# Four PSUM banks for the coarse exponentials, and four moved pieces, in a state-space convolution and feed-forward block

## The chip, the core and the metric

The kernel runs on one core of a Trainium2 chip. A core has TensorE (PE in the profile; PEld is its weight load), VectorE (DVE), ScalarE (ACT), GpSimd (POOL) and SyncE (SP), which issues the DMA transfers here. Each engine takes its instructions in the order of the program, and engines wait for one another on semaphores. TensorE writes to PSUM, which has eight banks of 128 partitions by 512 float32. The metric is the device time of one execution in microseconds (us); lower is better.

## The reference, cut to what matters

Two blocks in a row, each with a layer norm whose shift, scale and gate come from a small modulation vector:

```
mod = silu(c) @ w_mod                      # sa, ca, ga, sb, cb, gb
h = layernorm(x) * (1 + ca) + sa
x = x + ga * (S4 convolution of h)         # 512 channels, 2048 steps
h = layernorm(x) * (1 + cb) + sb
x = x + gb * (mish(h @ w1 + b1) @ w2)      # 512 -> 1792 -> 512
```

The convolution kernel of a channel is K[l] = Re sum over n of C[n] dB[n] exp(dt A[n] l), n = 0..127, l = 0..2047, with complex A, B, C. The output is the causal convolution of K with h, plus a skip term h * Dskip. It is computed with transforms over the 2048 steps; the transformed input is multiplied with the transformed K, and the product is transformed back. Mish is x * tanh(softplus(x)). All of it is in float32.

## The kernel before, in words

The program has three stages. The first, up to about 270 us, builds K for 512 channels and the transform of the normalised input. The second, up to about 365 us, multiplies the transforms and goes back. The third is the feed-forward block on TensorE, to the end. The change is in the first stage alone.

**Parameters.** The 512 channels make four blocks of 128 (b = 0..3). `params(b, stage)` turns a block's A, B, C, dt into the logarithm of a magnitude and an angle for every pole (lines 233-298); it runs on DVE, but for a logarithm and an exponential (stage 1) and an arctangent (stage 4) on ACT. Stage 5 writes the result, split in a rounded part and a rest, to the tile `pk`, of which there is one; `store_pk(b)` sends it to DRAM, and `load_s(b)` (line 546) brings it back in another layout: `S3` (magnitudes, one buffer) and two parts of `S12` (angles, three slots). Blocks 0, 1 and 2 are prepared ahead of the loop, block 3 inside it.

**Chunks.** A block is eight chunks of 16 channels, k = 0..31. For a chunk the kernel needs exp(z l) for 32 fine and 64 coarse values of l. The pieces of a chunk, with their names in the code and in the trace:

- `coarse(k, h)`, h = 0, 1: one product of 64x512 on PE (`pco`) into a PSUM bank, and its exponential on ACT into `co`. All 16 of a block are done in one go, `visit(b)`, since the exponential and the sines need different ACT tables. A visit is: load the exponential's table, 16 times product and exponential, load the sines' table.
- `s_ang` (PE, `pang`, 8 products) and `s_sin` (ACT, three passes: absolute value, sine, cosine) give the sines and cosines of the fine values in `ec`.
- `s_mag` and `comb` (DVE) multiply them with the magnitudes. `s_mag` is one 128x512 product into `m`. `comb` is four operations on `ec`: a product of 128x1024 with `co`, two of 128x512 with `m`, and one of 128x992 with `co`.
- `s_kgen` (PE, `pkg`, 64 small products into a bank), `s_ks` (ACT, a copy to `ks`), `s_skip` (DVE, adds the skip term to 4 columns of `ks`), `s_ka` (PE, `pka`, 16 products), `s_tm` (ACT, a copy to `gk`).

**The input's side.** The steps come in eight tiles of 256 (n = 0..7). `u_load` loads one, `u_stats(n)` (n even) takes the mean and variance of two tiles: 20 DVE operations (four statistics of 128x512, four aggregations, twelve of 128x4 for the inverse root). `u_norm(n)` is four DVE operations of 128x512, `u_mm` and `u_out` are products on PE (`pua`) and copies on ACT.

**The order.** It is written by hand: `follow` chains every instruction of PE, DVE, ACT and the SP loads in the order in which the code issues them. The loop (line 639) does at step k, on PE: `s_kgen(k-1)`, `s_ang(k+3)`, `s_ka(k-3)`, and what the table `pe` adds; on ACT and SP: `s_ks(k-1)`, what the table `se` adds, `s_sin(k+2)`, `s_tm(k-3)`; on DVE: the list `own`, between whose members the operations of the table `ve` ("extras") are spread evenly, and then those of `vt`. Calls such as `at(ve, 11, params, 3, 5)` fill the tables. `own` was:

```
own = comb(k) if 0 < k < NG else []
own.insert(1, lambda: step(s_skip, k - 2))
if k % 8 != 7:
    own.append(lambda: step(s_mag, k + 1))
```

so that the skip addition of chunk k-2 was the second DVE operation of step k. `s_kgen(k)` runs one step after `comb(k)` and needs all four of its operations. After steps 7, 15 and 23 comes the next visit; visit 0 is ahead of the loop.

**PSUM.** The eight banks are divided by tag: `pa` two pairs (`pang`), `pu` two single banks, `pb` two single banks. Before, all `pco` and `pua` take `pu`, while `pkg`, `pka` and `pmod` take `pb`. During a visit no other product runs on PE.

Of the kernel before, what the change touches and what calls it, by code (L numbers as in the profile page):

```python
# [10 lines left out]
F32 = mybir.dt.float32  # L11
F32R = mybir.dt.float32r
# [6 lines left out]
P = 128  # L19
# [65 lines left out]
def s4_block(ctx, tc, io, out):  # L85
# [9 lines left out]
    pre = p0.enter_context(tc.tile_pool(name="pre", bufs=1))  # L95
# [3 lines left out]
    psum = ps.enter_context(tc.tile_pool(name="psum", bufs=2, space=bass.MemoryType.PSUM))  # L99
# [3 lines left out]
    def follow(eng, ins):  # L103
        if eng in order:
            tc.add_manual_dep(ins.ins, order[eng].name,
                              mybir.DependencyInfo(mybir.DependencyClass.NoSync, mybir.DependencyReason.DATA),
                              reason="program order")
        order[eng] = ins.ins
# [31 lines left out]
    def act(out, in_, f, **kw):  # L140
        follow("act", nc.scalar.activation(out, in_, f, **kw))  # L141

    def tables(name):
        follow("act", nc.scalar.preload_act_table_set(name))

    def mm(out, lhsT, rhs, start=True, stop=True):
        follow("pe", T.matmul(out, lhsT, rhs, start=start, stop=stop))  # L147

    def load(dst, src):
        follow("sp", nc.sync.dma_start(dst, src))  # L150

    pkd = dram.tile([NB, P, 12 * P], F32, name="pkd")
# [4 lines left out]
    def pair(tag, name, bufs=None):  # L157
        return psum.tile([P, 2, 512], F32, tag=tag, name=name, **({"bufs": bufs} if bufs else {}))
# [4 lines left out]
    def view(src, offset, ap):  # L163
        return bass.AP(tensor=src.tensor, offset=src.offset + offset, ap=ap)
# [14 lines left out]
    def load_params(b):  # L179
        raw[b] = gen.tile([P, 16, P], F32, tag="raw" if b % 2 else "ec", name=f"raw{b}", bufs=1 if b % 2 else 3)  # L180
        load(raw[b][:, 0:6, :], io["par"][b].rearrange("p (k n) -> p k n", k=6))
# [118 lines left out]
    CO, S3 = {}, {}  # L300

    def coarse(k, h):
        if h == 0:
            CO[k] = gen.tile([P, 16, NM], F32, tag="co", name=f"co{k}", bufs=9)
        p = psum.tile([P, 512], F32, tag="pu", name=f"pco{k}{h}")
        mm(p[:, :8 * NM], S3[k // 8][:, k % 8, :], mc[:, h, :])
        act(CO[k][:, 8 * h:8 * h + 8, :].rearrange("p d x -> p (d x)"), p[:, :8 * NM], AF.Exp)

# [3 lines left out]
    def s_ang(k, half=None):  # L312
        if half != 1:
            PA[k] = pair("pa", f"pang{k}")
        s = S12[k // 4 % 3][:, k % 4]
        for e in range(2) if half is None else (half,):
            for n in range(4):
                rhs = ac[:, n // 3, :] if n % 3 == 0 else am[:, n - 1:n].to_broadcast([96, 512])
                mm(PA[k][:, e, :], s[:, e, :], rhs, start=(n == 0), stop=(n == 3))

    def s_sin(k):
        EC[k] = gen.tile([P, 2, 16, 96], F32, tag="ec", name=f"ec{k}", bufs=3)
        pv = PA[k].rearrange("p e (d x) -> p e d x", d=16)
        ang = [EC[k][:, z].rearrange("p d (e x) -> p e d x", x=32)[:, 0:3:2] for z in range(2)]
        A.activation(ang[0], pv, AF.Abs)
        act(ang[1], pv, AF.Sin, scale=-TWO_PI)
        act(ang[0], ang[0], AF.Sin, scale=-TWO_PI, bias=halfpi)
# [121 lines left out]
    def u_stats(n):  # L449
        v = Later()  # L450
        s6 = conv.tile([P, 4, 6], F32, tag="bst", name="bst", bufs=2)
        for h in range(4):
            v.bn_stats(s6[:, h], XT[n + h // 2][:, h % 2])
        for h in range(4):
            v.bn_aggr(mv[:, 2 * n + h, :], s6[:, h])
        rsqrt(rstd[:, 2 * n:2 * n + 4], mv[:, 2 * n:2 * n + 4, 1], 4, conv, "rsq", v)
        return v.ops
# [59 lines left out]
    def run(*lists):  # L517
        for i in range(max(map(len, lists))):
            for ops in lists:
                if i < len(ops):  # L520
                    ops[i]()
# [21 lines left out]
    def store_pk(b):  # L543
        load(pkd[b], PKR[b].rearrange("p i e n -> p (i e n)").bitcast(F32))

    def load_s(b):
        S3[b] = pre.tile([64, 8, P], F32R, tag="s3", name=f"s3_{b}")
        load(S3[b].bitcast(F32), view(pkd, P * b * 12 * P + 2 * P, [[3 * P, 64], [16 * 12 * P, 8], [1, P]]))
        for h in range(2):
            load(S12[(2 * b + h) % 3][0:64].bitcast(F32),  # L550
                 view(pkd, (P * b + 64 * h) * 12 * P, [[3 * P, 64], [16 * 12 * P, 4], [1, 2 * P]]))

    store_pk(0)
    load_s(0)
    for k in range(0, KB, 2):
        load(early[:, k:k + 2], view(io["w_mod"], k * P * 6 * D, [[6 * D, P], [P * 6 * D, 2], [1, 3 * D]]))
# [12 lines left out]
    def step(f, *a):  # L569
        if f.__name__[:2] == "s_":  # L570
            if (f, *a) in done or not 0 <= a[0] < NG:
                return
            done.add((f, *a))
            if a[1:] == (1,):
                done.add((f, a[0]))
        f(*a)

    def visit(b, others={}):
        tables("natural_log_exp_and_others")
        for i in range(16):  # L580
            coarse(8 * b + i // 2, i % 2)
            run(others.get(i, []))
        if b == 1:
            run(params(3, 1))
        tables("trig_and_small")

    s_ang(0)
    s_ang(1)
    s_sin(0)
    run(params(1, 4), params(2, 4))  # L590
    s_sin(1)
    run(params(1, 5))
    store_pk(1)
    load_params(3)
    run(params(2, 5))
    visit(0, {2: [lambda: step(s_mag, 0), lambda: run(comb(0))], 4: [lambda: step(s_mag, 1)]})
    store_pk(2)
    s_ang(2)
# [2 lines left out]
    pe, se, ve, vt = {}, {}, {}, {}  # L601

    def at(d, k, f, *a):
        d.setdefault(k, []).append((f, *a))

    at(pe, 0, mod_mm)
    at(se, 1, mod_out)
    at(ve, 1, u_stats, 0)
    at(ve, 3, gains)
    for b in range(NB - 1):  # L610
        at(se, 8 * b + 1, load_s, b + 1)
# [1 line left out]
    at(ve, 5, params, 3, 2)  # L613
    at(ve, 9, params, 3, 3)
    at(se, 11, run, params(3, 4))
    at(ve, 11, params, 3, 5)
    at(se, 12, store_pk, 3)
    for n, k, d in ((0, 4, ve), (1, 7, vt), (2, 10, ve), (3, 12, ve), (4, 15, vt), (5, 17, ve), (6, 20, ve), (7, 23, vt)):
        if n % 2 == 0 and n:
            at(ve, 8 if n == 2 else k - 1, u_stats, n)  # L620
# [18 lines left out]
    for k in range(NG + 1):  # L639
        tc.cur_priority = 100000 + 10000 * k  # L640
        for s in [(s_kgen, k - 1), (s_ang, k + 3), (s_ka, k - 3)] + pe.get(k, []):
            step(*s)
        for s in [(s_ks, k - 1)] + se.get(k, []) + [(s_sin, k + 2), (s_tm, k - 3)]:
            step(*s)
        own = comb(k) if 0 < k < NG else []
        own.insert(1, lambda: step(s_skip, k - 2))
        if k % 8 != 7:
            own.append(lambda: step(s_mag, k + 1))
        extra = [o for f, *a in ve.get(k, []) for o in f(*a)]
        for i, o in enumerate(own):  # L650
            o()
            for e in extra[len(extra) * i // len(own):len(extra) * (i + 1) // len(own)]:
                e()
        for f, *a in vt.get(k, []):
            run(f(*a) or [])
        if k % 8 == 7 and k + 1 < NG:
            visit(k // 8 + 1)
            step(s_mag, k + 1)
# [23 lines left out]
    psum = ps.enter_context(tc.tile_pool(name="psum1", bufs=2, space=bass.MemoryType.PSUM))  # L682
# [59 lines left out]
    psum = ps.enter_context(tc.tile_pool(name="psum2", bufs=4, space=bass.MemoryType.PSUM))  # L742
# [163 lines left out]
```

## Time and profile before

| | us |
|---|---|
| median of three runs (lowest, highest) | 733.49 (732.96, 736.34) |
| the profiled execution, its own time | 735.84 |
| its span, first to last instruction | 734.1 |
| outside the span | 1.74 |

| busy in the span | PE | DVE | ACT |
|---|---|---|---|
| 734.1 us | 648.6 | 412.4 | 323.7 |

Times of rows are us from the start of the span. A row of the timeline is: start, duration, engine, line, operation, what is written from what is read, shapes, how many instructions are merged into it; in brackets the idle time of that engine just before, and who ended it. Nearly all rows of the first stage have the line of a helper (L119, L141, L147, L150), so tiles tell them apart. PEclk is the share of the full TensorE clock that was granted; in this trace it is 1.0 or 0.5, in pieces of about 3.4 us.

The four visits are at 38 to 50 us, 95 to 107, 158 to 170 and 215 to 227, by ACT's rows of `co`.

### The profile page before, as it was taken

The page shows a single profiled execution, that of the slowest core. Times are in us where ns is not written, and L with a number is a line of the kernel's source. Part 1 is how long each engine was busy: PE and PEld are TensorE (multiplying, and loading weights), DVE is VectorE, ACT ScalarE, POOL GpSimd, SP SyncE. Part 2 cuts the span into 40 slices and gives each one's busy share as a digit, 9 for nine tenths or more (in the row PEclk, how much of TensorE's full clock was granted, in tenths as well). Part 3 has the DMA queues.
Part 4 walks back from the last instruction along what each step waited for, and adds up shares of the span by engine and source line. Part 5 has one row for each costly group of instructions (what it writes and reads, how often), then busy time and mean ns, then how long its engine had stood idle before and what let it go on. Part 6 is the DMA issues. An engine that isn't in the chain of part 4 may idle for free.

```text
span 734.1 us, 11767 instructions
## 1 busy us (share of the span) xinstructions
PE 648.6 (88%) x4848; PEld 437.5 (60%) x4848; DVE 412.4 (56%) x813; ACT 323.7 (44%) x466; POOL 5.0 (1%) x12
## 2 busy tenths in 40 slices
PE   0489879889979988999737999999999999999996
PEld 0246646546646752333206877887788877888884
DVE  8788978996884837786548224432424324431113
ACT  2477687687986863353305312322123222322220
POOL 2000000000000000000000000000000000000000
PEclk9959958887985999999976999999999999999998
DMA  7841123522423268995275522032500500010002
GB/s 188 272 136 61 45 71 104 188 87 77 142 88 115 100 178 251 300 298 182 115 200 171 116 57 58 1 65 50 114 1 1 115 0 1 0 40 19 0 1 58
DMA packets 34313, 74.62 MB, mean 102 GB/s; under 512 B 5418, under 2 KB 9902, under 8 KB 33748
## 3 DMA queue, kind: packets, MB, share of 16 engines
q1 hardware_dynamic: 33380, 72.17, 33.9%
q10 hardware_dynamic: 576, 1.05, 0.7%
q0 software_dynamic: 304, 0.66, 0.4%
q8 instruction: 38, 0.62, 0.4%
q14 instruction: 15, 0.12, 0.1%
HBM read 49.73 MB, written 24.13 MB: 101 GB/s over the span
## 4 chain that ended last, share of the span: by engine, by line
PE 50%; DVE 3%; DMA 2%; issue 0%; ACT 0%; SPq 0%; DVEq 0%; ACTq 0%
PE pm L795 22%; PE po L812 21%; PE pz L147 2%; PE pia L760 2%; PE pub L147 2%; PE pkb L147 1%; DMA zl<-zd 1%; PE pln L780 1%; DVE ot L119 1%; DVE y L119 0%; DVE w2l L119 0%; DMA zd<-z 0%; DVE x L119 0%; DMA out<-ot 0%; DVE rsq L119 0%
## 5 line engine op out<-in xcount | busy, mean ns | idle before, releaser
L795 PE MATMUL pm<-hh,w1h 128*128 128x512 f32 x448 | 143.2, 400 | 0.7 <-ACT hh L119 0.7
L141 ACT ACTIVATE mh<-pm,b 128x512 f32<-128x512 f32 x56 | 38.6, 689 | 229.7 <-PE pm L795 229.7
L119 DVE TENSOR_TENSOR mal<-mh,mah 128x512 fp32r<-128x512 f32 x56 | 38.7, 691 | 156.8 <-ACT mah L119 156.4
L795 PEld LDWEIGHTS pm<-hh,w1h 128*128 128x128 f32 x448 | 85.3, 190 | 21.8 <-ACT hh L119 1.5
L812 PE MATMUL po<-w2h,mah 128*128 128x512 f32 x224 | 89.4, 399 | 0.0
L795 PE MATMUL pm<-hh,w1l 128*128 128x512 f32 x224 | 89.3, 399 | 0.0
L812 PE MATMUL po<-w2l,mah 128*128 128x512 f32 x224 | 88.6, 395 | 0.0
L812 PE MATMUL po<-w2h,mal 128*128 128x512 f32 x224 | 88.5, 395 | 0.0
L147 PE MATMUL pang<-ac,s 96*128 96x512 f32 x128 | 55.0, 476 | 27.2 <-DMA s<-pkd 27.2
L119 DVE TENSOR_TENSOR ec<-ec,co 128x1024 f32<-128x1024 f32 x64 | 76.9, 1201 | 1.8 <-ACT ec L141 1.8
L147 PE MATMUL pco<-mc,s 64*128 64x512 f32 x64 | 39.8, 708 | 17.1 <-ACT co L141 17.1
L119 DVE TENSOR_TENSOR y<-pkb,f 128x1024 f32<-128x1024 f32 x32 | 37.7, 1219 | 25.1 <-PE pkb L147 25.1
L147 PEld LDWEIGHTS pkg<-ec 128*32 128x32 f32 x2048 | 34.9, 114 | 28.2 <-issue 18.9
L812 PEld LDWEIGHTS po<-w2h,mah 128*128 128x128 f32 x224 | 42.1, 188 | 14.6 <-ACT mah L119 4.9
L147 PEld LDWEIGHTS pang<-ac,s 96*128 96x128 f32 x128 | 28.6, 224 | 34.7 <-issue 27.6
L795 PEld LDWEIGHTS pm<-hh,w1l 128*128 128x128 f32 x224 | 42.6, 190 | 10.1
L812 PEld LDWEIGHTS po<-w2h,mal 128*128 128x128 f32 x224 | 42.1, 188 | 10.2
L812 PEld LDWEIGHTS po<-w2l,mah 128*128 128x128 f32 x224 | 42.1, 188 | 9.8
L147 PE MATMUL pkg<-ec 128*32 128x64 f32 x2048 | 39.6, 230 | 7.1 <-DVE ec L119 5.3
L147 PE MATMUL pang<-am,s 96*128 96x512 f32 x128 | 45.3, 441 | 0.0
L147 PEld LDWEIGHTS pco<-mc,s 64*128 64x128 f32 x64 | 16.9, 269 | 38.9 <-ACT co L141 38.0
L141 ACT ACTIVATE co<-pco 128x512 f32<-128x512 f32 x64 | 35.5, 595 | 10.2 <-PE pco L147 9.5
(97 smaller groups left out, 863.0 us busy)
## 6 DMA issues: line engine op xcount, KB each, us to landing
ud<-u SPq DMA_DIRECT2D x16, 512.0 KB, 3.4
ur<-ud SPq DMA_DIRECT2D x32, 256.0 KB, 4.5
zd<-z SPq DMA_DIRECT2D x16, 512.0 KB, 4.0
zl<-zd SPq DMA_DIRECT2D x28, 256.0 KB, 4.9
x<-in_A_u SPq DMA_DIRECT2D x32, 128.0 KB, 3.3
x<-in_A_u SPq DMA_DIRECT2D x8, 512.0 KB, 6.6
out<-ot SPq DMA_DIRECT2D x32, 128.0 KB, 2.3
w1s<-in_B_w SPq DMA_DIRECT2D x8, 448.0 KB, 6.5
```

Of the source, the lines that this page charges most:

```text
L119: ins = getattr(self.engine, name)(*a, **kw)
L141: follow("act", nc.scalar.activation(out, in_, f, **kw))
L147: follow("pe", T.matmul(out, lhsT, rhs, start=start, stop=stop))
L760: T.matmul(p[64 * tl:64 * tl + 64, :], di, ZL[tt, hv][:, j % 2, tl, :], start=True, stop=True)
L780: T.transpose(p[:, P * q:P * q + P], LNX[tt, q][:, P * b:P * b + P], ident)
L795: T.matmul(p, w1[wi][:, k, fs], hh[:, hi, k, :], start=(n == 0), stop=(n == 3 * KB - 1))
L812: T.matmul(PO[tt][q], a[ai][:, P * q:P * q + P], w2[wi][:, f, :], start=(f == 0 and n == 0), stop=(f == FB - 1 and n == 2))
```

## The change

Five edits, all in the first stage.

1. `coarse(k, h)` takes a bank of the tag `pb` for even k, and of `pu` for odd k. A visit's products go round four banks in place of two.
2. `load_s` issues the two loads of `S12` ahead of the load of `S3`.
3. Ahead of the loop, the arctangents of blocks 1 and 2 stand before `s_sin(0)` on ACT, and no more between `s_sin(0)` and `s_sin(1)`.
4. `u_stats(0)` runs ahead of visit 0, as a whole, and no more between the operations of step 1. The last stage of block 3's parameters (`params(3, 5)`) and its store move one step later, from 11 and 12 to 12 and 13.
5. In `own`, the last operation of `comb` (128x992) becomes the second, and the skip addition comes after all four operations of `comb`.

```
 def coarse(k, h):
-    p = psum.tile([P, 512], F32, tag="pu", name=f"pco{k}{h}")
+    p = psum.tile([P, 512], F32, tag="pu" if k % 2 else "pb", name=f"pco{k}{h}")
...
 def load_s(b):
-    S3[b] = pre.tile([64, 8, P], F32R, tag="s3", name=f"s3_{b}")
-    load(S3[b].bitcast(F32), ...)
     for h in range(2):
         load(S12[(2 * b + h) % 3][0:64].bitcast(F32), ...)
+    S3[b] = pre.tile([64, 8, P], F32R, tag="s3", name=f"s3_{b}")
+    load(S3[b].bitcast(F32), ...)
...
 s_ang(1)
+run(params(1, 4), params(2, 4))
 s_sin(0)
-run(params(1, 4), params(2, 4))
 s_sin(1)
...
 run(params(2, 5))
+run(u_stats(0))
 visit(0, ...)
...
-at(ve, 1, u_stats, 0)
...
-at(ve, 11, params, 3, 5)
-at(se, 12, store_pk, 3)
+at(ve, 12, params, 3, 5)
+at(se, 13, store_pk, 3)
...
 own = comb(k) if 0 < k < NG else []
-own.insert(1, lambda: step(s_skip, k - 2))
+if own:
+    own.insert(1, own.pop())
+own.append(lambda: step(s_skip, k - 2))
```

**First place: ACT ahead of visit 0.** Here `raw1` and `raw2` are the parameters of blocks 1 and 2 (their arctangent), `pang0` and `ec0` the angles and sines of chunk 0. Before:

```order
L119 ACTIVATE ec0_302<-pang0_284 128x2x16x32
L141 ACTIVATE ec0_302<-pang0_284 128x2x16x32
L141 ACTIVATE ec0_302<-ec0_302,halfpi_100 128x2x16x32
L141 ACTIVATE raw1_152<-raw1_152 128x128
L141 ACTIVATE raw2_154<-raw2_154 128x128
L119 ACTIVATE ec1_308<-pang1_293 128x2x16x32
```

and now:

```order
L141 ACTIVATE raw1_152<-raw1_152 128x128
L141 ACTIVATE raw2_154<-raw2_154 128x128
L119 ACTIVATE ec0_304<-pang0_284 128x2x16x32
L141 ACTIVATE ec0_304<-pang0_284 128x2x16x32
L141 ACTIVATE ec0_304<-ec0_304,halfpi_100 128x2x16x32
L119 ACTIVATE ec1_308<-pang1_293 128x2x16x32
```

The two arctangents stand ahead of the first sines.

**Second place: DVE around chunk 1.** `x0`, `x1` are the tiles of the input, `bst`, `mv`, `rsq` and `rstd` belong to `u_stats(0)`, `m2_1` is chunk 1's `m`. Before:

```order
L119 TENSOR_TENSOR m2_1_354<-co1_337 128x512
L119 TENSOR_TENSOR ec1_308<-ec1_308,co1_337 128x32x32
L119 BN_STATS bst_486<-x0_201 128x6 x2
L119 BN_STATS bst_486<-x1_206 128x6 x2
L119 BN_AGGR mv_134<-bst_486 128x2 x2
L119 TENSOR_TENSOR ec1_308<-ec1_308,m2_1_354 128x16x32
L119 BN_AGGR mv_134<-bst_486 128x2 x2
L119 TENSOR_SCALAR rsq_487<-mv_134 128x4
L119 TENSOR_SCALAR rstd_135<-rsq_487 128x4
L119 SCALAR_TENSOR_TENSOR ec1_308<-ec1_308,m2_1_354 128x16x32
```

and now, with the statistics ahead of `m2_0`, further up:

```order
L119 TENSOR_TENSOR m2_1_377<-co1_360 128x512
L119 TENSOR_TENSOR ec1_308<-ec1_308,co1_360 128x32x32
L119 TENSOR_TENSOR ec1_308<-ec1_308,co1_360 128x32x31
L119 TENSOR_TENSOR ec1_308<-ec1_308,m2_1_377 128x16x32
L119 SCALAR_TENSOR_TENSOR ec1_308<-ec1_308,m2_1_377 128x16x32
L119 TENSOR_TENSOR m2_2_513<-co2_373 128x512
```

Nothing is left between the four operations of `comb(1)`; the 20 of `u_stats(0)` are now in front of the first operation that needs `co`.

**Third place: DVE at steps 11 and 12.** `raw3` and `pk3` are block 3's parameters, which wait for the arctangent that ACT does at step 11; `ks9` is the skip addition. Before:

```order
L119 TENSOR_TENSOR ec11_1164<-ec11_1164,co11_967 128x32x32
L119 SCALAR_TENSOR_TENSOR raw3_320<-raw3_320 128x128
L119 TENSOR_TENSOR ks9_1242<-ks9_1242,dtap_86 128x4
L119 SCALAR_TENSOR_TENSOR raw3_320<-raw3_320 128x128
L119 TENSOR_TENSOR ec11_1164<-ec11_1164,m2_11_1266 128x16x32
L119 TENSOR_SCALAR raw3_320<-raw3_320 128x128
L119 SCALAR_TENSOR_TENSOR ec11_1164<-ec11_1164,m2_11_1266 128x16x32
L119 SCALAR_TENSOR_TENSOR raw3_320<-raw3_320 128x128
L119 TENSOR_TENSOR ec11_1164<-ec11_1164,co11_967 128x32x31
L119 CAST pk3_1341<-raw3_320 128x3x2x128
```

and now:

```order
L119 TENSOR_TENSOR ec11_1164<-ec11_1164,co11_967 128x32x32
L119 TENSOR_TENSOR ec11_1164<-ec11_1164,co11_967 128x32x31
L119 TENSOR_TENSOR ec11_1164<-ec11_1164,m2_11_1266 128x16x32
L119 SCALAR_TENSOR_TENSOR ec11_1164<-ec11_1164,m2_11_1266 128x16x32
L119 TENSOR_TENSOR ks9_1242<-ks9_1242,dtap_86 128x4
L119 TENSOR_TENSOR m2_12_1337<-co12_974 128x512
L119 TENSOR_TENSOR ec12_1253<-ec12_1253,co12_974 128x32x32
L119 SCALAR_TENSOR_TENSOR raw3_320<-raw3_320 128x128
L119 TENSOR_TENSOR ec12_1253<-ec12_1253,co12_974 128x32x31
L119 SCALAR_TENSOR_TENSOR raw3_320<-raw3_320 128x128
```

The operations on `raw3` stand one step further down, the skip addition behind the four of `comb`.

More of the change, by code (lines that the diff above doesn't have):

```diff
@@ L546, in load_s @@
     def load_s(b):
-        S3[b] = pre.tile([64, 8, P], F32R, tag="s3", name=f"s3_{b}")
-        load(S3[b].bitcast(F32), view(pkd, P * b * 12 * P + 2 * P, [[3 * P, 64], [16 * 12 * P, 8], [1, P]]))
         for h in range(2):
@@ L551, in load_s @@
                  view(pkd, (P * b + 64 * h) * 12 * P, [[3 * P, 64], [16 * 12 * P, 4], [1, 2 * P]]))
+        S3[b] = pre.tile([64, 8, P], F32R, tag="s3", name=f"s3_{b}")
+        load(S3[b].bitcast(F32), view(pkd, P * b * 12 * P + 2 * P, [[3 * P, 64], [16 * 12 * P, 8], [1, P]]))
     store_pk(0)
```

## The prediction

> **What bounds the kernel now.** I read the page's busy shares first, then TensorE's waits, then the windows by clock, then the timeline around a visit.
>
> ```profile
> PE 648.6 (88%) x4848; PEld 437.5 (60%) x4848; DVE 412.4 (56%) x813; ACT 323.7 (44%) x466; POOL 5.0 (1%) x12
> ```
>
> TensorE sets the end. The windows by stage say where it does not run at its best:
>
> ```profile
> 95.20:115.70 20.50, 18.20 (x106) 10.29 (x106) 16.89 (x46) 14.76 (x25) 0.00 (x0) 0.50 0.16 39
> ...
> 139.50:146.40 6.90, 6.90 (x32) 3.96 (x34) 6.90 (x11) 4.51 (x7) 0.00 (x0) 0.51 0.72 227
> ...
> 160.00:173.70 13.70, 13.66 (x83) 7.17 (x84) 7.72 (x12) 11.85 (x19) 0.00 (x0) 0.50 0.16 39
> ...
> 214.60:235.10 20.50, 17.86 (x106) 10.29 (x106) 10.20 (x14) 14.58 (x23) 0.00 (x0) 0.50 0.29 103
> ...
> 390.00:734.00 344.00, 335.59 (x1448) 263.12 (x1448) 117.27 (x217) 90.05 (x138) 0.00 (x0) 0.98 0.19 43
> ```
>
> After the length come PE's, PEld's, DVE's, ACT's and POOL's busy time, then the granted clock. From 390 us PE is busy for 335.6 of 344 us: nothing of the change is there, and that part only moves as a block. In the visits the clock is half. The waits from 34 us to 260 us, and the timeline of visit 1:
>
> ```profile
> ACT co L141 <- PE pco L147: 9.5, 27, 0.4
> DVE raw L119 <- ACT raw L141: 7.4, 2, 4.3
> PE pkg L147 <- DVE ec L119: 5.3, 4, 1.9
> ```
>
> ```profile
> 95.65 1.08 ACT L141 ACTIVATE co<-pco 128x512 f32<-128x512 f32 x2
> 97.13 1.08 ACT L141 ACTIVATE co<-pco 128x512 f32<-128x512 f32 x2 [0.39 <-PE pco L147]
> ...
> 106.01 1.09 ACT L141 ACTIVATE co<-pco 128x512 f32<-128x512 f32 x2 [0.40 <-PE pco L147]
> ...
> 105.18 1.28 PE L147 MATMUL pco<-mc,s 64*128 64x512 f32 x2 [0.20 <-ACT co L141]
> 106.39 1.96 PE L147 MATMUL pkg<-ec 128*32 128x64 f32 x64
> ...
> 109.72 1.06 PE L147 MATMUL pang<-ac,s 96*128 96x512 f32 x2
> 110.58 1.05 PE L147 MATMUL pang<-am,s 96*128 96x512 f32 x2
> ...
> 115.81 1.17 PE L147 MATMUL pkg<-ec 128*32 128x64 f32 x64
> 120.98 1.17 PE L147 MATMUL pkg<-ec 128*32 128x64 f32 x64
> ```
>
> With two banks the two engines take turns: a pair of exponentials every 1.48 us (97.13 - 95.65), of which ACT works 1.09 and waits 0.39 for products that could only begin when a bank was read. Between visits a chunk takes 5.17 us at the full clock (120.98 - 115.81) and 9.42 at half (115.81 - 106.39), without a gap on PE.
>
> **Edit 1, four banks.** An exponential of mean 595 ns in pairs of 1.09 starts every 0.49 us. At half clock products of 512 columns follow one another at 0.43 us ((110.58 - 109.72) / 2): PE can keep ACT fed when it may be four ahead. So 16 exponentials take 15 x 0.49 + 0.60 = 8.0 us instead of 106.01 + 1.09 - 95.65 = 11.45: ACT leaves 3.5 earlier. PE's last product now needs the 12th exponential, not the 14th: it ends 6.75 us after the first exponential's start (11 x 0.49 + 0.60, a 0.1 hand-over, 0.65 for the product) instead of 10.74 (106.39 - 95.65): **4.0 per visit** on PE. Below, this term is bounded by 0: for even k the bank is shared with `pkg` and `pka`, and `s_tm` must have read it. That copy stands right ahead of the table load, whose 1.28 us cover it here; if they did not, the ring would start a product late. Above, 4.0 plus what a full clock would bring (rivals).
>
> A rule speaks against this term: the Trainium skill, TensorE: Matmul & The Clock Gate, section "HAM oscillation — how this bites in real kernels", reports that adding PSUM double-buffering to a kernel of its own gave no further gain. By that, edit 1 is worth 0 and the time is that of the second rival; the 27 waits of 0.39 above say otherwise.
>
> **Edits 2 and 3, ahead of visit 0.**
>
> ```profile
> 22.00 1.95 SPq L150 DMA_DIRECT2D s<-pkd  x3
> ...
> 29.53 0.35 DVE L119 TENSOR_SCALAR raw<-raw 128x128 f32<-128x128 f32 x2
> 30.95 1.02 ACT L119 ACTIVATE ec<-pang 128x1024 f32<-128x1024 f32 x1 [8.49 <-PE pang L147]
> 33.82 0.51 ACT L141 ACTIVATE raw<-raw 128x128 f32<-128x128 f32 x2
> 34.16 0.62 DVE L119 SCALAR_TENSOR_TENSOR raw<-raw 128x128 f32<-128x128 f32 x2 [4.27 <-ACT raw L141]
> 34.22 1.02 ACT L119 ACTIVATE ec<-pang 128x1024 f32<-128x1024 f32 x1
> 38.50 1.09 ACT L141 ACTIVATE co<-pco 128x512 f32<-128x512 f32 x2
> ```
>
> One load issue is 0.65 us (1.95 / 3), so the first angles come up to 0.65 earlier. The arctangents' input is ready at 29.88, so they end at 30.4, while ACT still waits for angles; the sines start there, 0.55 earlier, and the 0.40 between the two chunks' sines (33.82 to 34.22) falls away. Gain 0.95 (0.4 if the load lands no earlier). The later `load_s` calls I cost at 0: their angles are used four and more steps later. On SP the last such load now waits for block 3's store, with two loads of `w_mod` behind it that have ten steps' time.
>
> **Edit 4, the statistics.** DVE gets the arctangents at 30.4 instead of 34.16 and is done with the parameters 3.7 earlier, at 39.6 instead of 43.3; then come the 20 operations of `u_stats(0)`. Interleaved, they cost 4.6 (below: 8.78 - 4.17); in one piece, where each small one waits for the one before, I take 5.3. So the first `s_mag` starts at 44.9, 1.6 later than before.
>
> ```profile
> 43.29 0.68 DVE L119 TENSOR_TENSOR m<-co 128x512 f32<-128x512 f32 x1
> ...
> 56.76 1.22 DVE L119 TENSOR_TENSOR ec<-ec,co 128x1024 f32<-128x1024 f32 x1
> ...
> 60.51 0.17 DVE L119 TENSOR_TENSOR ks<-ks,dtap 128x4 f32<-128x4 f32 x1 [2.19 <-ACT ks L119]
> ...
> 71.43 1.22 DVE L119 TENSOR_TENSOR ec<-ec,co 128x1024 f32<-128x1024 f32 x1
> ...
> 78.20 1.22 DVE L119 TENSOR_TENSOR ec<-ec,co 128x1024 f32<-128x1024 f32 x1
> ...
> 76.50 1.16 PE L147 MATMUL pkg<-ec 128*32 128x64 f32 x64 [1.88 <-DVE ec L119]
> ...
> 88.42 1.17 PE L147 MATMUL pkg<-ec 128*32 128x64 f32 x64
> ```
>
> From there DVE needs 56.76 - 43.29 - 4.6 = 8.9 to chunk 2's first product: 53.8. To chunk 4's it took 14.67, of which 2.19 was the skip addition waiting for a copy; edit 5 puts that wait behind the products, where the copy is there. 53.8 + 12.5 = 66.3, 5.1 earlier than 71.43. That step takes 6.77 (78.20 - 71.43); the chunk's four products end some 4.7 into it (the rest are the operations behind them), at 71.0, and `pkg` of chunk 4 starts there and not at 76.50. PE, ahead by 0.95 and 4.0, comes there at 69.7 at the latest (76.50 - 1.88 - 4.95), so it waits 1.3 or more for DVE. The next products are done at 66.3 + 6.77 + 4.2 = 77.3, and with one more chunk of PE, 5.17, `pkg` of chunk 6 starts at 82.5 and not at 88.42: **5.9** (5.3 if the clock drops to half after that wait, as in the window at 139.5).
>
> **Edit 5 and the arctangent of block 3, between visits 1 and 2.**
>
> ```profile
> 97.38 1.22 DVE L119 TENSOR_TENSOR ec<-ec,co 128x1024 f32<-128x1024 f32 x1
> ...
> 109.35 0.17 DVE L119 TENSOR_TENSOR ks<-ks,dtap 128x4 f32<-128x4 f32 x1 [1.57 <-ACT ks L119]
> ...
> 127.42 0.29 DVE L119 SCALAR_TENSOR_TENSOR raw<-raw 128x128 f32<-128x128 f32 x1 [3.14 <-ACT raw L141]
> ...
> 138.00 1.15 PE L147 MATMUL pkg<-ec 128*32 128x64 f32 x64 [1.94 <-DVE ec L119]
> ...
> 139.70 1.22 DVE L119 TENSOR_TENSOR ec<-ec,co 128x1024 f32<-128x1024 f32 x1
> 143.87 1.22 DVE L119 TENSOR_TENSOR ec<-ec,co 128x1024 f32<-128x1024 f32 x1
> ...
> 151.52 1.17 PE L147 MATMUL pkg<-ec 128*32 128x64 f32 x64
> 152.65 1.23 DVE L119 TENSOR_TENSOR ec<-ec,co 128x1024 f32<-128x1024 f32 x1
> ```
>
> A plain step is 4.17 on DVE, one with statistics 8.78. PE gains 5.9 + 4.0 = 9.9 by the end of visit 1. DVE starts chunk 8 when two exponentials are done, so 5.9 earlier, at 91.5, and goes to chunk 14 in 46.49 less the waits of 1.57 and 3.14: 133.3. Chunk 14's four products with 10 statistics among them take 6.7: 140.0. PE would be there at 137.7, so **DVE bounds this stretch**: the gain at `pkg` of chunk 14 is 151.52 - 140.1 = 11.4, and the stall of 1.94 before it becomes stalls of some 1.2 and 2.3. Half clock after such a stall cost the chunk at 138.00 some 146.4 - 138.0 - 5.17 = 3.2 (the second window above); I charge 1.3 and keep 0 to 3.2. Gain at visit 2: **10.1**.
>
> **Sum.** From visit 2 on PE hardly waits for DVE: of the four waits, 5.3 us in all, 1.88 and 1.94 lie before, so at most 1.5 is left. Visits 2 and 3 bring 4.0 each. 10.1 + 8.0 = 18.1, so 735.84 - 18.1 = 717.7 for an execution like the profiled one. The median of the runs is 2.35 below it, 733.49, and I say **717**; my own range is 712 to 722.
>
> **Rivals.** *The clock stays full after the visits.* Products every 0.49 us at 0.43 each are 87% of PE's time; before, two in 1.48 were 58%. If that is enough activity, the chunk after visit 3 takes 5.2 and not 9.4, and about half as much is won after visit 2, where half clock ended at 173.7, sooner after the visit: 6.3 more, 711. Against it: after visit 1 PE ran without a gap from 106.39 and still had half clock until 115.7. The Trainium skill, TensorE: Matmul & The Clock Gate, section "What's actually happening", says the full clock comes after one busy window of 3.4 us; by that this rival wins, but here it took 9.3 us.
>
> *The banks bring nothing*: the ring is held by the shared `pb` banks, or ACT's pace is not the limit. Visits stay at 11.45; edits 2 to 5 remain. PE without its early stalls is 5.7 ahead at visit 1, DVE bounds chunk 14 at 140.3, a gain of 11.2, and no more comes: 735.84 - 11.2 = 724.6. For it: DVE bounds two stretches whatever the visits do.
>
> *Slower, through the clock.* With DVE the bound, PE stalls by about 2 us in chunk after chunk, and each such stall is followed by a chunk at half clock: 3.2 to 4.2 each. That outweighs the 18.1 from the sixth chunk on (18.1 / 3.2); at ten chunks of 3.7 it is 735.84 - 18.1 + 37 = 755. Against it: PE at half clock is slower than DVE's 4.2 to 8.8 per step, so it stops waiting and the clock returns, as at 146.4.
>
> **Chances.** Forecast 0.60, full clock 0.13, banks bring nothing 0.18, in between that and no change 0.05, slower 0.04. A difference of 0.5% (3.7 us) is about what can be told from none: faster 0.91, same 0.05, slower 0.04. The range goes from a little below the full-clock case to above the bank rival: 709 to 727.
>
> **What would show it.** In the new profile ACT's `co` rows in a visit should follow without waits, 16 in 8.0 us; the first `co` should start near 37.5, `m` of chunk 0 near 44.9; DVE should no more wait 3.14 for `raw`, and PE should wait for DVE near chunks 4, 13 and 14. I am wrong if a visit's `co` rows still have gaps of 0.39, if the windows between 115 and 160 are mostly at half clock, or if the stage from 390 us on does not simply move forward.

## The result, and the profile after

| | before | after |
|---|---|---|
| median of four runs (lowest, highest), us | 734.24 (732.96, 736.34) | 715.66 (714.55, 718.41) |
| the profiled execution, us | 735.84 | 714.55 |
| its span, us | 734.1 | 712.8 |
| its mean granted clock | 0.923 | 0.941 |

The ratio is 0.9767, with a 95% interval from 0.9736 to 0.9797: 18.6 us faster; 717 us was forecast and 715.66 measured. The two profiled spans lie further apart, by 21.3 us, because the one of before was 1.6 us above its median and the one of after 1.1 us below.

The busy shares of the changed kernel:

```profile
PE 634.3 (89%) x4848; PEld 432.8 (61%) x4848; DVE 412.8 (58%) x813; ACT 319.9 (45%) x466; POOL 5.0 (1%) x12
```

The instructions are as many as before. PE's busy time fell by 14.3 us, with a smaller part of it at half clock. The windows of the changed kernel, with the same columns as before (length; busy PE, PEld, DVE, ACT, POOL; granted clock; DMA share; GB/s), show four stretches at half clock and the rest of the program:

```profile
89.60:99.90 10.30, 9.75 (x80) 6.60 (x81) 9.01 (x26) 10.24 (x21) 0.00 (x0) 0.50 0.01 2
134.00:140.80 6.80, 6.80 (x28) 4.01 (x26) 6.59 (x22) 4.54 (x7) 0.00 (x0) 0.50 0.53 171
147.60:157.90 10.30, 9.41 (x81) 6.06 (x80) 9.24 (x13) 10.26 (x20) 0.00 (x0) 0.50 0.03 13
202.30:215.90 13.60, 13.60 (x101) 8.79 (x101) 11.29 (x16) 10.88 (x18) 0.00 (x0) 0.50 0.44 155
370.00:712.80 342.80, 334.47 (x1448) 262.27 (x1448) 117.16 (x216) 90.14 (x138) 0.00 (x0) 0.99 0.19 43
```

Half clock still goes with every visit, but for 10.3, 10.3 and 13.6 us instead of 20.5, 13.7 and 20.5. The last row is the block that only moves: 1448 products as before, 334.5 us of PE against 335.6.

The waits of the changed kernel from 34 to 160 us on DVE, and of PE from 96 to 142 us (total, times, longest):

```profile
DVE pk L119 <- DMA pkd<-pk: 4.1, 1, 4.1
DVE m L119 <- ACT co L141: 2.9, 2, 1.8
```

```profile
PE pkg L147 <- DVE ec L119: 3.5, 4, 1.9
```

DVE's waits for `raw` (3.14 at one place) and for `ks` are gone from this part: from the end of the first wait, at 38.3, to 160 us DVE waits 2.9 us in all. ScalarE's rows in visits 0 and 1:

```profile
37.17 7.95 ACT L141 ACTIVATE co<-pco 128x512 f32<-128x512 f32 x16
```

```profile
88.20 1.28 ACT L144 ACT_TABLE_LOAD   x1
89.50 7.94 ACT L141 ACTIVATE co<-pco 128x512 f32<-128x512 f32 x16
97.14 0.83 ACT L141 ACTIVATE raw<-raw 128x128 f32<-128x128 f32 x2
```

All 16 exponentials of a visit merge into one row without a wait. PE in the same visit, and the chunks behind it:

```profile
90.15 6.18 PE L147 MATMUL pco<-mc,s 64*128 64x512 f32 x12 [0.95 <-ACT co L141]
96.25 1.95 PE L147 MATMUL pkg<-ec 128*32 128x64 f32 x64
...
103.02 1.17 PE L147 MATMUL pkg<-ec 128*32 128x64 f32 x64
...
132.03 0.27 PE L147 MATMUL pkg<-ec 128*32 128x64 f32 x2 [1.90 <-DVE ec L119]
...
140.91 1.17 PE L147 MATMUL pkg<-ec 128*32 128x64 f32 x64
```

The points that the prediction named, in us from the start of the span (predicted values that the text gave only as a gain are worked out from it):

| | before | predicted | after |
|---|---|---|---|
| first exponential of visit 0 | 38.50 | 37.5 | 37.17 |
| first `m` | 43.29 | 44.9 | 45.23 |
| `pkg` of chunk 4 | 76.50 | 71.0 | 69.64 |
| `pkg` of chunk 6 | 88.42 | 82.5 | 82.27 |
| `pkg` of chunk 14 | 151.52 | 140.1 | 140.91 |
| first product of visit 2 | 155.64 | 145.5 | 145.03 |
| `pkg` of chunk 16, behind visit 2 | 176.47 | 162.4 | 161.36 |
| `pkg` of chunk 24, behind visit 3 | 235.41 | 217.3 | 216.18 |
| end of the span | 734.1 | 716.0 | 712.8 |

### The profile page after: what moved, and what is told of

It reads as the page before. It is cut to its first block, busy times and chain, and to the rows that moved or that the text cites. A ratio compares the mean times of both kernels' runs of the same rounds, so it can differ in the third digit from the quotient of the medians.

```text
span 712.8 us, 11831 instructions
## 1 busy us (share of the span) xinstructions
PE 634.3 (89%) x4848; PEld 432.8 (61%) x4848; DVE 412.8 (58%) x813; ACT 319.9 (45%) x466; POOL 5.0 (1%) x12
## 4 chain that ended last, share of the span: by engine, by line
PE 69%; DVE 21%; ACT 4%; DMA 3%; issue 2%; SPq 0%; ACTq 0%; DVEq 0%
PE pm L797 22%; PE po L814 22%; DVE ec L119 8%; PE pub L147 4%; PE pz L147 4%; DVE raw L119 4%; PE pkb L147 4%; PE pang L147 3%; PE pkg L147 2%; PE pka L147 2%; PE pia L762 2%; PE pco L147 2%; DVE x L119 1%; PE pua L147 1%; ACT ec L141 1%
## 5 line engine op out<-in xcount | busy, mean ns | idle before, releaser
L797 PE MATMUL pm<-hh,w1h 128*128 128x512 f32 x448 | 142.5, 398 | 0.6 <-ACT hh L119 0.6
L119 DVE TENSOR_TENSOR ec<-ec,co 128x1024 f32<-128x1024 f32 x64 | 75.0, 1204 | 8.4 <-ACT ec L141 8.4
L147 PE MATMUL pang<-ac,s 96*128 96x512 f32 x128 | 53.2, 461 | 25.8 <-DMA s<-pkd 25.8
L147 PE MATMUL pkg<-ec 128*32 128x64 f32 x2048 | 42.0, 230 | 7.6 <-DVE ec L119 6.7
L814 PEld LDWEIGHTS po<-w2h,mal 128*128 128x128 f32 x224 | 42.1, 188 | 10.2
L147 PE MATMUL pang<-am,s 96*128 96x512 f32 x128 | 43.5, 425 | 0.0
L147 PE MATMUL pco<-mc,s 64*128 64x512 f32 x64 | 30.4, 624 | 11.2 <-ACT co L141 7.1
L141 ACT ACTIVATE ec<-ec,halfpi 128x1024 f32<-128x1024 f32 x32 | 37.5, 1173 | 0.0
L147 PE MATMUL pka<-bdk,ks 128*64 128x128 f32 x512 | 36.5, 288 | 0.9 <-ACT gk L119 0.9
```

Source lines behind the costliest of these rows:

```text
L119: ins = getattr(self.engine, name)(*a, **kw)
L797: T.matmul(p, w1[wi][:, k, fs], hh[:, hi, k, :], start=(n == 0), stop=(n == 3 * KB - 1))
L814: T.matmul(PO[tt][q], a[ai][:, P * q:P * q + P], w2[wi][:, f, :], start=(f == 0 and n == 0), stop=(f == FB - 1 and n == 2))
```

## The experiments

The theory: the two-bank ring sets the pace of a visit, and four banks take 4.0 us off each; the small edits start VectorE's chain of products earlier; VectorE then bounds the stretch between visits 1 and 2. The rivals: the banks bring nothing, the gains simply add, or one of the small edits carries much of it. Each ratio is against the kernel before, timed on the same chip beside it. Four runs of one kernel lie 1.5 to 7 us apart, so differences of 2 us between two variants are not told apart by their times; where such a difference is read, it is read from starts in the traces. A trace is of one execution, and starts scatter too: the changed kernel and the three variants below that differ from it only behind visit 1 start that visit at 86.39, 86.60, 87.13 and 87.13 us.

### The banks alone, and everything but the banks

The kernel before with edit 1, and the changed kernel without it:

```
-p = psum.tile([P, 512], F32, tag="pu", name=f"pco{k}{h}")
+p = psum.tile([P, 512], F32, tag="pu" if k % 2 else "pb", name=f"pco{k}{h}")
```

> The kernel before with edit 1 alone: the coarse products go over the four banks of both rings, all else as before. Theory (the two-bank ring set the pace of a visit, 0.86 us a tile instead of the exponential's own 0.49): a visit loses 4.0 us of PE time, three later visits sit on PE's path, 12.0; with earlier visits VectorE's products wait longer for skip and arctangents, which gives a part back or adds a little: 720 to 722, a gain of 12 to 14.5. Rival (the banks bring nothing, because ScalarE or the clock sets a visit): 734.

> The changed kernel with edit 1 undone: a visit's tiles on the two banks of one ring, all other edits kept. Theory of the prediction (banks 4.0 a visit on PE's path, 16.0 in all, but VectorE bounds the stretches from visit 0 and visit 1 on, so that 4.0 to 8.0 of it is hidden there): 723 to 728. Rival (the gains simply add, the banks were worth all 16.0 of the 18.6): 731.7. Rival (banks bring nothing): 715.7.

| | median, us | ratio to before, 95% |
|---|---|---|
| banks alone | 721.64 | 0.9824 (0.9806 to 0.9841) |
| all but the banks | 728.41 | 0.9914 (0.9894 to 0.9934) |
| changed kernel | 715.66 | 0.9767 (0.9736 to 0.9797) |

ScalarE in visit 1 with the banks alone, and the waits from 34 to 260 us and a part of visit 1 without them:

```profile
92.46 7.95 ACT L141 ACTIVATE co<-pco 128x512 f32<-128x512 f32 x16
```

```profile
ACT co L141 <- PE pco L147: 9.3, 25, 0.4
```

```profile
99.47 1.09 ACT L141 ACTIVATE co<-pco 128x512 f32<-128x512 f32 x2 [0.39 <-PE pco L147]
100.94 1.09 ACT L141 ACTIVATE co<-pco 128x512 f32<-128x512 f32 x2 [0.39 <-PE pco L147]
```

The banks alone bring 12.8 us, at the foot of the 12 to 14.5 expected, and the wait of 0.39 per pair comes and goes with them. That settles the rival "the banks bring nothing". Without the banks 6.0 us are left; the 728.41 lies just above the 723 to 728 expected. The two gains add up to 18.8, almost the whole 18.6, so by the times they simply add (the 731.7 of that rival is missed because the banks are worth 12.8 here, not 16.0). But the traces show that they are not independent. The starts of the kernel without the banks, less those of the changed kernel:

| visit 1 | `pkg` 8 | `pkg` 12 | `pkg` 14 | visit 2 | visit 3 | `pkg` 24 |
|---|---|---|---|---|---|---|
| 4.3 | 10.2 | 8.9 | 2.5 | 3.5 | 9.8 | 13.1 |

By chunk 8 the banks are worth 10.2 us (two visits and what goes with the clock), and at chunk 14 only 2.5 are left: in the changed kernel PE arrives early and waits for DVE, 3.5 us above, and loses 3.7 at half clock behind the longest wait. VectorE's bound, with the half clock behind it, took 7.7 us, as the theory says. The last two visits give 3.7 each again; another 2.6 is won behind visit 2, where half clock ends sooner, and 0.4 lost behind visit 3. Added to the kernel before, the banks lose nothing ahead of visit 2: chunk 8 starts 7.3 us earlier, visit 2 7.2, visit 3 9.5 and chunk 24 13.9. The banks' gain comes by two different ways to about the same end, so the sum that fits is no proof that the parts do not touch each other.

### Three banks

```
-tag="pu" if k % 2 else "pb"
+tag="pb" if (2 * k + h) % 3 == 2 else "pu"
```

> The changed kernel with a visit's coarse products over three banks: every third on the one ring, which has two buffers, in an order that comes back to a bank after three products at the soonest. Theory (a bank is busy for about 1.5 us, product plus exponential plus what lies between, and the exponentials follow each other every 0.49, so that three are just enough): 715.7 to 717.7. Rival (a bank is held for longer, only four hide it): 3 to 7 us more, 719 to 723.

It took 717.70 us, ratio 0.9776 (0.9752 to 0.9801). ScalarE in its visit 2:

```profile
146.55 7.98 ACT L141 ACTIVATE co<-pco 128x512 f32<-128x512 f32 x16
```

The products on `pu` come back to their bank after three products; the ring `pb` has two buffers in turn, so every third product comes back to its bank only after six. ScalarE runs as fast with this order as with four banks. PE leaves a visit 0.5 later (10.4 us from its first product to its last, not 9.9), as it can be one product less ahead; the times do not tell this half microsecond. A bank used again after three products is thus soon enough, for two products of three; a ring of three banks and no more was not run.

### The arctangents back between the sines

```
 s_ang(1)
-run(params(1, 4), params(2, 4))
 s_sin(0)
+run(params(1, 4), params(2, 4))
 s_sin(1)
```

> The changed kernel with edit 3 undone: the arctangents of blocks 1 and 2 again between the sines of chunks 0 and 1. Theory (their place is worth little to ScalarE, 0.4 to 0.55 at the first exponential, but some 3 to VectorE, which does the parameters and then the statistics behind them): first exponential of visit 0 at 37.6, first m at 48.0 to 48.5 instead of 45.2, chunk 4's small products and visit 1 some 3 later, since VectorE bounds the stretch between; 717.5 to 719.5 at the end. Rival (VectorE waits for the store of its parameters in any case): first m within 0.6 of 45.2, 716.

It took 719.86 us (716.34 to 720.86), ratio 0.9808 (0.9788 to 0.9827), just above the 717.5 to 719.5 expected. Its interval overlaps that of the changed kernel, and the trace is of its fastest run. Its VectorE ahead of visit 0, and below it that of the changed kernel:

```profile
32.57 0.62 DVE L119 SCALAR_TENSOR_TENSOR raw<-raw 128x128 f32<-128x128 f32 x2 [3.10 <-ACT raw L141]
...
39.83 0.95 DVE L119 CAST pk<-raw 128x768 fp32r<-128x768 f32 x1 [2.96 <-DMA pkd<-pk]
...
46.74 0.69 DVE L119 TENSOR_TENSOR m<-co 128x512 f32<-128x512 f32 x1
```

```profile
29.97 0.62 DVE L119 SCALAR_TENSOR_TENSOR raw<-raw 128x128 f32<-128x128 f32 x2 [0.30 <-ACT raw L141]
...
38.33 0.95 DVE L119 CAST pk<-raw 128x768 fp32r<-128x768 f32 x1 [4.05 <-DMA pkd<-pk]
...
40.19 2.46 DVE L119 BATCH_NORM_STATS2 bst<-x 128x6 f32<-128x512 f32 x4
...
45.23 0.69 DVE L119 TENSOR_TENSOR m<-co 128x512 f32<-128x512 f32 x1
```

Neither theory is right: the first `m` comes 1.5 later, not 3 and not 0. Of the 2.6 us by which the arctangents now come earlier, 1.1 go into a longer wait for the store of block 1, which has to leave the one `pk` tile. What is left travels: `pkg` of chunk 4, visit 1 and visit 3 each start 1.5 later than in the changed kernel. (Visit 2 starts 2.8 later; here half clock begins ahead of it, at 142.5 and not at 147.6.) For ScalarE the edit is worth nothing: the first exponential is at 36.91 here and at 37.17 in the changed kernel. The earlier start is edit 2's. In every kernel with it the first `pang` starts between 25.4 and 26.1, in the two without it (before, and the banks alone) at 27.2 and 27.3; each of the other edits was undone alone, and the early start stayed.

### Three small edits undone one at a time

The statistics back in the loop; the old order of `own`; block 3's last parameters back at steps 11 and 12:

```
-run(u_stats(0))
 ...
+at(ve, 1, u_stats, 0)
```

```
-if own:
-    own.insert(1, own.pop())
-own.append(lambda: step(s_skip, k - 2))
+own.insert(1, lambda: step(s_skip, k - 2))
```

```
-at(ve, 12, params, 3, 5)
-at(se, 13, store_pk, 3)
+at(ve, 11, params, 3, 5)
+at(se, 12, store_pk, 3)
```

> The changed kernel with the first statistics back in step 1 of the loop, all else kept. Theory (VectorE bounds the stretch up to chunk 6 with the same sum of work wherever the statistics stand, and ahead of the loop they cost the first chunk what they free later): 715.2, 1.0 either way. Rival (ahead of the loop they stand in VectorE's idle wait and so free the loop of 5.0 us): 719 to 721.

> The changed kernel with edit 5 undone: in a chunk of own products the skip addition stands second and the 128x992 product last, as before. Theory (the skip row is there in time with the arctangents moved ahead, so the order moves no work): 716.5, 0 to 1.5 more than the changed kernel's 715.7. Rival (the order itself carries part of the gain, because skip's transfer is late behind a visit): 719 or more.

> The changed kernel with block 3's second arctangents and the store behind them back at step 11 and 12. Theory (they stand at VectorE's list ahead of chunk 14's products or in the stretch before it, and TensorE at half clock covers a part): 717, 0 to 2 more than 715.7. Rival (VectorE bounds all of this stretch, and what was moved past the visit comes back in full): about 719 to 724.

| undone | median, us | ratio to before, 95% | visit 1 starts | visit 2 starts |
|---|---|---|---|---|
| nothing (changed kernel) | 715.66 | 0.9767 (0.9736 to 0.9797) | 86.39 | 145.03 |
| statistics ahead of the loop | 718.00 | 0.9779 (0.9763 to 0.9795) | 86.15 | 143.62 |
| order of `own` | 717.41 | 0.9774 (0.9759 to 0.9789) | 86.53 | 145.93 |
| block 3's step | 713.22 | 0.9710 (0.9688 to 0.9732) | 86.60 | 143.81 |

The first two cannot be told from the changed kernel by their intervals; that of the third lies just below. For the statistics 715.2 was expected, and 719 to 721 by the rival; 718.00 lies between and settles neither by itself. Their place moves visit 1 by 0.24 us, less than the scatter above, which fits VectorE's bound: the sum of its work up to chunk 6 is the same. PE's waits with the old order, from 96 to 145 us, against the 3.5 above:

```profile
PE pkg L147 <- DVE ec L119: 5.0, 4, 1.7
PE pkg L147 <- DVE rstd L119: 2.4, 1, 2.4
```

So the order does take 3.9 us of waits off PE there, but only 0.9 arrive at visit 2, and the time does not show it. Block 3's step was expected to cost 0 to 2 when put back; the median is 2.4 lower, so the move did not help. What matters for the prediction is that the wait for `raw` does not come back. DVE's list of waits from 34 to 260 us with the step undone:

```profile
DVE ec L119 <- ACT ec L141: 8.6, 5, 3.1
DVE y L119 <- PE pkb L147: 7.4, 1, 7.4
DVE ks L119 <- ACT ks L119: 6.0, 4, 3.7
DVE pk L119 <- DMA pkd<-pk: 4.4, 1, 4.4
DVE m L119 <- ACT co L141: 4.3, 2, 2.5
DVE bst L119 <- DMA x<-in_A_u: 1.6, 1, 1.6
```

There is no row for `raw`, though the operations stand where they stood. With earlier visits DVE is the late one, and by the time it asks for the arctangent ScalarE has done it. These are ScalarE's arctangent and VectorE's first operation behind it in this kernel:

```profile
115.09 0.31 ACT L141 ACTIVATE raw<-raw 128x128 f32<-128x128 f32 x1
```

```profile
116.62 0.29 DVE L119 SCALAR_TENSOR_TENSOR raw<-raw 128x128 f32<-128x128 f32 x1
```

With the banks alone, 0.8 of the 3.1 us is left. The move was not needed for the wait to go.

### VectorE's bound ahead of visit 2, relieved

If VectorE bounds the stretch between the visits, work that can wait should go behind visit 2. Chunk 15's products are needed only after it, so what stands in step 15 is hidden by the visit.

The first kernel moves the statistics of block 4 from step 14 to 15:

```
-at(ve, 8 if n == 2 else k - 1, u_stats, n)
+at(ve, {2: 8, 4: 15, 6: 19}[n], u_stats, n)
```

The second has this and block 3's last parameters with their store later:

```
-at(ve, 12, params, 3, 5)
-at(se, 13, store_pk, 3)
+at(ve, 15, params, 3, 5)
+at(se, 16, store_pk, 3)
```

The third has both, and two pieces from ahead of visit 1 next to it:

```
-at(ve, 2, params, 3, 0)
-at(ve, 5, params, 3, 2)
+at(ve, 7, params, 3, 0)
+at(ve, 7, params, 3, 2)
```

> The changed kernel with block 4's statistics one step later, behind the visit instead of ahead of it. Theory (VectorE bounds the stretch between visits 1 and 2, and the statistics are 3.3 us of it): 712.4. Rival (TensorE's own work, at half clock before that visit, bounds it): 715.7, no change.

> The changed kernel with two blocks moved behind visit 2 instead of ahead of it: block 4's statistics (as in the run before) and block 3's second arctangents with their store (step 15 and 16). Theory (what is left of VectorE's bound ahead of visit 2 is the one stall of 1.8 at chunk 13): 710, at most 1.8 below the 711.9 of the statistics alone. Rival (TensorE's own work sets all of that stretch once the statistics are out): 711.9, no change. Rival (the later store makes block 3's angles late for visit 3): 714 or more.

> The same two blocks behind visit 2, and two more pieces of block 3's arctangents and ranges from steps 2 and 5 to step 7, next to visit 1. Theory (ahead of visit 1 VectorE is what chunks 4 and 5 wait for, 0.8 to 1.8, and between visits 1 and 2 the moved pieces take the place of those moved on): 708 to 710. Rival (the pieces now lie ahead of the products that the chunks after visit 1 need, and the stall only moves there): 711 to 714.

| | median, us | ratio to before, 95% | visit 1 | visit 2 | visit 3 |
|---|---|---|---|---|---|
| changed kernel | 715.66 | 0.9767 (0.9736 to 0.9797) | 86.39 | 145.03 | 197.03 |
| statistics of block 4 behind visit 2 | 711.93 | 0.9705 (0.9667 to 0.9742) | 87.13 | 142.54 | 195.18 |
| and block 3's last parameters | 710.89 | 0.9681 (0.9639 to 0.9723) | 87.13 | 140.13 | 193.51 |
| and two pieces from ahead of visit 1 | 710.11 | 0.9683 (0.9652 to 0.9714) | 84.11 | 138.26 | 194.83 |

PE's waits from 96 to 142 us in the first and in the second of them:

```profile
PE pkg L147 <- DVE ec L119: 2.1, 2, 1.8
```

```profile
PE pco L147 <- ACT gk L119: 1.3, 1, 1.3
```

The 3.5 us of waits for DVE become 2.1, and then none. This is the bound shown directly: with less of VectorE's work ahead of visit 2, that visit starts 2.5 and 4.9 us earlier. The last variant moves work from ahead of visit 1 as well: visit 1 starts 2.3 us earlier than in the changed kernel, and visit 2 6.8. It gives part of that back between visits 2 and 3, where PE waits 1.8 for the copy `gk` ahead of chunk 20's small products and loses a chunk at half clock behind it. Its interval lies below that of the changed kernel, without overlap: about 5.6 us faster than it, 24 faster than the kernel before. So does that of the second; that of the first overlaps it a little. The three are not told apart from one another.

### What brings the clock down in a visit

Every coarse product issued twice; and, in another kernel, one more product over all 128 rows ahead of each coarse product of visits 1 to 3:

```
-mm(p[:, :8 * NM], S3[k // 8][:, k % 8, :], mc[:, h, :])
+for _ in range(2):
+    mm(p[:, :8 * NM], S3[k // 8][:, k % 8, :], mc[:, h, :])
```

```
+if k > 7:
+    mm(p[:, :8 * NM], fl[:, 0:P], fl[:, 0:1].to_broadcast([P, 8 * NM]))
 mm(p[:, :8 * NM], S3[k // 8][:, k % 8, :], mc[:, h, :])
```

> The changed kernel with every coarse product issued twice into the same bank, so that TensorE has about no gaps in a visit; the work is repeated and nothing is left out. Theory (gaps of TensorE in a visit take its clock down, and gapless work brings it back within 4 to 10 us): full clock soon after or already in the visit, a visit 1 to 2 us longer, about 721. Rival (the clock falls at a visit whatever TensorE does there): 16 tiles at 0.85 us, 5.7 more a visit, about 738.

> The changed kernel with one more product ahead of each coarse product of visits 1 to 3, into the same bank, over all 128 rows (ones by ones; the coarse product then overwrites it, nothing is left out). Theory (TensorE's clock follows how much of the array works, and the coarse product's 64 rows are too few): full clock through the visits, they stay at 9.9, 705 to 712. Rival (the clock falls at a visit whatever is issued there, as with the coarse products issued twice, 17 us at half clock each time): 727 to 731.

One execution each: 730.87 and 737.01 us. The windows of the first, in visit 1 (with the stretch ahead of half clock and the one behind the visit), 2 and 3:

```profile
91.00:95.80 4.80, 3.44 (x16) 1.92 (x13) 2.56 (x5) 4.77 (x8) 0.00 (x0) 1.00 0.32 121
95.80:104.60 8.80, 8.80 (x21) 6.38 (x20) 8.52 (x26) 6.67 (x12) 0.00 (x0) 0.50 0.01 2
104.60:112.90 8.30, 8.30 (x91) 6.30 (x92) 8.02 (x22) 6.22 (x9) 0.00 (x0) 0.50 0.11 28
...
153.80:162.10 8.30, 8.30 (x20) 5.86 (x19) 8.28 (x12) 6.38 (x12) 0.00 (x0) 0.50 0.01 2
211.90:220.00 8.10, 8.10 (x20) 5.88 (x18) 7.44 (x10) 6.22 (x12) 0.00 (x0) 0.50 0.01 2
```

and those of the second, visits 1, 2 and 3:

```profile
90.00:109.00 19.00, 19.00 (x31) 7.48 (x32) 12.15 (x32) 8.42 (x15) 0.00 (x0) 0.50 0.00 0
...
158.20:174.60 16.40, 16.40 (x27) 6.38 (x30) 9.00 (x13) 6.81 (x12) 0.00 (x0) 0.50 0.00 0
217.20:231.70 14.50, 13.56 (x40) 5.99 (x41) 10.07 (x14) 11.72 (x19) 0.00 (x0) 1.00 0.07 28
```

With doubled products PE has no gap for 8 us and more, nor in the chunk behind visit 1, and the clock stays at half all the while, 17.1 us in all each time. So the gaps between the products are not what keeps the clock down, and the theory of activity, taken as PE's busy time, falls. It does not show that gaps have no part in bringing the clock down: it fell 4.7 us after the visit's first product, and in these PE was busy for 3.4 of 4.8 us. (The rival's 738 was too much: with two products in 0.85 us at half clock a visit is 13.4 to 13.6 us long, some 3.6 more than 9.9, where 5.7 more were charged.) The Trainium skill, TensorE: Matmul & The Clock Gate, section "What's actually happening", gives full clock after one busy window of some 3.4 us; the stretches at half clock here, busy for more than two such windows in a row, disagree. The same section calls the windows free-running, and with that the traces agree: stretches at half clock last 3.4, 6.8, 10.2, 13.7, 17.1, 20.5 or 27.3 us, all multiples of 3.41 (but for a stretch that the end of the trace cuts short), and where they begin relative to a visit changes from kernel to kernel.

With products over all rows neither expectation is met. Visits 1 and 2 ran at half clock but for their first 3.4 and 5.0 us, 22.5 and 21.3 us long, and visit 3 at full clock from end to end, 14.5 long. Twice half clock tells against the rows as the whole cause, and once full clock tells against a clock that falls at every visit. What decides it stays open.

## Why the prediction was right

**Edit 1, four banks: right in kind and size.** ScalarE's 16 exponentials take 7.94 us (8.0 predicted), and PE goes from the first product of visit 1 to its last in 9.93 instead of 13.92: 4.0, as said. The lower bound of 0, a shared bank that is not yet read, did show up as a wait, but in front of the first exponential: PE waits 1.3 for `gk` in each of the three later visits, and the table load covers it. The rule that was weighed against the term (the Trainium skill, TensorE: Matmul & The Clock Gate, "HAM oscillation — how this bites in real kernels": double-buffering in PSUM gave that kernel no further gain) did not carry over: the banks alone are worth 12.8 us here.

**Edits 2 and 3: the sum nearly right, the parts wrong.** The first exponential came 1.33 earlier, 0.95 predicted. The step gave up to 0.65 of it to the order of the loads and the rest to the arctangents. With the arctangents put back the first exponential stays where it is: all of it is the loads, which bring the first angles 1.4 earlier, twice what the step allowed them. The step counted the issue of a load, 0.65; in the trace the three loads are issued at this pace but land 1.3 to 1.4 apart (at 25.72, 27.03 and 28.42 before). The first `pang` started at 27.16, behind the second landing, and now starts at 25.78, behind the first, at 25.64. That the sum came out near is partly luck: the loads were taken too small and the arctangents' place too large.

**Edit 4, the statistics: right.** The block took 5.0 (40.19 to 45.2; 5.3 predicted), the first `m` came at 45.23 (44.9). What was not in the step is that VectorE, with its arctangents earlier, waits longer for the store of block 1 (4.05, not 2.97 as before), and so the statistics start at 40.19 instead of 39.6. Chunk 4's `pkg` started 1.4 earlier than predicted, because PE issues two of a `pkg`'s 64 products before it waits for VectorE's last operation. Chunk 4's other 62 start at 70.81, where 71.0 was said, and chunk 6 at 82.27, where 82.5 was:

```profile
69.64 0.27 PE L147 MATMUL pkg<-ec 128*32 128x64 f32 x2 [0.76 <-ACT gk L119]
70.81 1.15 PE L147 MATMUL pkg<-ec 128*32 128x64 f32 x62 [0.90 <-DVE ec L119]
```

**Edit 5 and block 3: the bound right, its reason half right.** This is VectorE around chunk 14's last product, and the chunk behind it:

```profile
139.03 0.68 DVE L119 SCALAR_TENSOR_TENSOR ec<-ec,m 128x512 f32<-128x512 f32 x1
...
141.97 2.33 DVE L119 TENSOR_TENSOR ec<-ec,co 128x1024 f32<-128x1024 f32 x2
```

VectorE's products for chunk 14 were done at 139.7 (140.0 predicted). PE came after that, at 140.91, since half clock behind the stall of 1.90 stretched chunk 13 to 8.9 us. (The stalls up to there make 3.5 us in all; the step had 1.2 and 2.3.) The clock cost chunk 13 3.7 us, a little over the upper bound of 3.2, but only the 1.2 by which PE then came later than VectorE count; 1.3 were charged. The step gives no working for its 1.3, so that it came so near is luck. The gain at visit 2 was 10.6 (10.1 predicted). The step took off the wait for `raw` together with the move of block 3's parameters; the run without that move has no such wait either.

**Visits 2 and 3, and the end.** 15.1 and 19.2 had been won behind visits 2 and 3 (14.1 and 18.1 predicted). Up to chunk 24 the sum is thus 1.1 short, 0.5 of it from before visit 2, and most of the rest from half clock, which ends sooner behind visit 2 than before. Another 2.1 came later, in stages that the change does not touch: 0.9 up to the feed-forward's first product (at 393.3 before and at 373.1 after), and 1.1 behind it. There half clock lasts to 399.0 before and to 376.3 after, 5.7 us of products against 3.2. The windows of the clock fall differently; no edit put them there, and no term of the sum has them.

**The rivals.** *The clock stays full* did not happen: half clock goes with every visit, and even products without gaps do not end it. A part of its gain is there all the same: half clock ended 3.6 us behind visit 1 and not 9.3, and 3.0 behind visit 2 and not 4.3; behind visit 3 it lasted 9.0 as before. *The banks bring nothing* is refuted, and its price was too good: edits 2 to 5 alone gave 6.0 us, not 11.2. The step that failed there is PE "5.7 ahead at visit 1": it was 1.8 ahead (90.73 against 92.54). Without the banks half clock still takes a window at 75.1 to 78.5, which stretches chunk 4 to 7.9 us where 5.2 is the full clock's: 2.7 of the 3.9 that are missing. *Slower, through the clock* was not seen: half clock followed one stall, the one of 1.90, not chunk after chunk.

## What to carry to other kernels

When two engines take turns through a small ring of buffers, write down the cycle of one buffer (here 1.48 us: product, exponential, two hand-overs) and divide it by the pace of the slower engine (0.49): the quotient, three, was the depth that kept ScalarE at its pace here, and idle buffers of another ring may serve. Then ask who is late next: here VectorE, and only the work moved off its list ahead of the next fixed point gave more time, while reordering within the list gave none that the times show. A wait that a change removes may be gone without it, once its engine has become the late one, so undo each part alone before crediting it.

## What the runs showed of the hardware that was not expected

- TensorE ran without a gap for 8.8, 8.3 and 8.1 us at half clock, when its products were the coarse ones issued twice; with products over all rows among them, one visit of three stayed at full clock. The cause was not found.
- With products over all rows and coarse products in turn, a product took 0.72 us at half clock (26 of them from 90.15 to 108.95 us) and 0.42 at full clock (visit 3). The coarse products issued twice, with the same weights four times in a row, started 0.43 us apart at half clock (18 steps from 96.39 to 104.07 us). Whether the change of weights or the rows make the difference was not separated.
